# Two more tiles transposed by a DMA out of DRAM instead of on TensorE, and what is loaded around them

## The chip, the cores and the metric

The kernel runs on one core of one Trainium2 chip. The metric is the device time of one execution in microseconds (us). The profile is of one execution, taken by the hardware profiler. Engines are named as the profile names them: PE is TensorE's matmuls and PEld its weight loads, DVE is VectorE, ACT is ScalarE, POOL is GpSimd, and SP is SyncE, which here only issues DMAs.

## The reference

One block of a token-mixing MLP on x of 2048 rows by 512 columns, bf16:

```python
h = gelu(layernorm(x) @ w1)                       # 512 -> 512
g0, g1, g2, g3 = four column quarters of h, shifted along the rows by +1, -1, +2, -2 (zeros come in)
x1 = x + concat(g0, g1, g2, g3) @ w2              # 512 -> 512
out = x1 + gelu(layernorm(x1) @ w3) @ w4          # 512 -> 1792 -> 512
```

The layer norms have no weights; gelu is the tanh approximation.

## The kernel before, in words

The 2048 rows are 16 tiles of 128 (row 16p + t is partition p of tile t, line 183), so a shift along the rows by 1 or 2 is mostly a shift from tile to tile. Weights, x and all stages stay in SBUF.

A matmul contracts over partitions, so each tile of x has to be transposed (`xnT`) ahead of the matmul with w1. There are two ways to the first layer:

- *Raw tiles*, 0 to 5 (R = 6, line 180). x itself is transposed, not its norm: on PE (`tp`, line 314, four 128x128 transposes a tile, copied out of PSUM by `ev` on ACT, line 328) for tiles 0 to 3, or by a DMA out of DRAM (`tdma_x`, line 349, two tiles in one DMA, named `tdx_`) for tiles 4 and 5. `m1r` (line 374) multiplies with w1, `rc` (line 387, ACT) copies the result to SBUF as `yraw`. The norm is made up for later: `zr` (line 391, DVE) takes off mean times the column sums of w1 (`cs`, line 363, copied out by `cse`, line 369), `g1r` (line 397, ACT) scales by rstd and applies gelu, and `tdma_h` (line 355, `th_`) transposes the result into `hT`.
- *Normed tiles*, 6 to 15. Statistics (`st`, line 286, then `ag`, line 292) and the norm (`nm`, line 304) are DVE's, the inverse root (`rs`, line 297) is POOL's. `xn` is transposed by a DMA out of SBUF (`tdma`, line 338, `td0_`; pairs 6, 12, 14) or on PE (`tp8`, `tp10`, pairs 8 and 10). `m1p` (line 404) multiplies two tiles at once, `g1p` or `g1s` (lines 417, 424) apply gelu into `hT`.

The second layer (`m2s`, line 444, and `m2`, line 429) reads the shifted neighbours of a tile in `hT`: the normed tiles 8 to 15 come first, and of the raw tiles they need only 0 and 1, in the last three matmuls of that group. `x1` (line 458, DVE) adds x. Tiles of x1 are normed, transposed by DMA (`td1_`) and go through w3 (`m3h`, line 484, and `m3`, line 464) and w4 (`m4`, line 507) in blocks of four tiles; `fin` (line 519) adds x1 and stores.

The statistics of the raw tiles are needed only by `zr` and `rs`, so they are spread over DVE's time; they read x as it was loaded, so each raw tile that is transposed out of DRAM is loaded as well (`load_x`, line 271, `ldx`).

Each operation is an `Op` with the resources that it reads and writes (line 35). `firsts` (lines 633 to 648) writes out the order of the operations on each engine by hand; whatever it doesn't name follows in the order of its creation. `arrange` (line 38) merges the five lists, `emit` (line 84) turns the dependences into semaphore waits. An engine goes through its list strictly in order, SP too: a DMA whose data isn't ready holds back those listed behind it. All loads and DMA transposes go through SP, except ldw10, ldw12 and ldx1, which ACT issues. PSUM banks are fixed by hand (tp0 to tp3 in banks 6 and 7, the column sums in bank 4, which `m1p8` uses next).

Of the kernel before, what the change touches and what calls it, by code (L numbers as in the profile page):

```python
# [171 lines left out]
def bass_standalone__mixer_s_mlp__prompt_kernel(nc: bass.Bass, x, w1, w2, w3, w4, out):  # L172
# [15 lines left out]
    with ExitStack() as es:  # L188
# [82 lines left out]
        def load_x(t, n, eng="sp"):  # L271
            add(eng, f"ldx{t}", lambda e: e.dma_start(x_sb[:, t : t + n, :], xd[:, t : t + n, :]),
                writes=[(("x", i), 0) for i in range(t, t + n)], dma=True)
# [40 lines left out]
        def tp(t, n, b, raw):  # L314
            src = x_sb if raw else xn
            rd = [(("x", i), 0) if raw else (("xn", i), 0) for i in range(t, t + n)]

            def f(e):
                ins = None
                for i in range(n):  # L320
                    for c in range(DC):
                        o = 1024 * b + (i * DC + c) * P
                        ins = e.transpose(psb[:, o : o + P], src[:, t + i, P * c : P * (c + 1)], ident[:])  # L323
                return ins

            add("pe", f"tp{t}", f, reads=rd + [("ident", 1)], writes=bres(b, 1, f"tp{t}"))

        def ev(t, n, b, eng="act"):
            src = psb[:, 1024 * b : 1024 * b + n * D]
            dst = xnT[:, t : t + n, :, :].rearrange("p t c s -> p (t c s)")  # L330
            if eng == "act":
                f = lambda e: e.activation(dst, src, ACT_F.Copy)  # L332
            else:
                f = lambda e: e.tensor_copy(dst, src)
            add(eng, f"ev{t}", f, reads=bres(b, 1, f"tp{t}"), writes=[(("xT", i), 0) for i in range(t, t + n)])
# [13 lines left out]
        def tdma_x(t):  # L349
            add("sp", f"tdx_{t}",  # L350
                lambda e: e.dma_start(xnT[:, t : t + 2, :, :].rearrange("p t c s -> p (t c) s"),
                                      xd[:, t : t + 2, :].rearrange("p t d -> p (t d)"), transpose=True),
                writes=[(("xT", i), 0) for i in (t, t + 1)], dma=True)
# [20 lines left out]
        def m1r(t, b, c0=0, c1=DC):  # L374
            def f(e):
                ins = None
                for c in range(c0, c1):
                    ins = e.matmul(bank(b), xnT[:, t, c, :], w1_sb[:, c, :], start=(c == 0), stop=(c == DC - 1))  # L378
                return ins

            rd = [(("xT", t), 0)] + W1[c0:c1]
            if c0:
                rd += bres(b, 1, f"m1r{t}{c0}")
            end = f"{c1}" if c1 < DC else ""
            add("pe", f"m1r{t}{end}", f, reads=rd, writes=bres(b, 1, f"m1r{t}{end}"))

        def rc(t, b):
            add("act", f"rc{t}", lambda e: e.activation(yraw[:, t, :], bank(b), ACT_F.Copy),
                reads=bres(b, 1, f"m1r{t}"), writes=[(("yraw", t), 0)])
# [168 lines left out]
        load_w1(2, "act")  # L558
        load_w1(3, "sp")
        load_x(1, 1, "act")  # L560
        for t, n in ((6, 1), (7, 1), (2, 1), (8, 1), (3, 1), (9, 1), (10, 1), (11, 1), (12, 1), (13, 1), (14, 1), (15, 1), (4, 2)):
            load_x(t, n)
        for c in range(DC):
            load_w2(c)
# [7 lines left out]
            colsum(4, c)  # L572
        colsum_out(4)
        for t in range(R):
            if t < 4:
                tp(t, 1, 6 + t % 2, True)
                ev(t, 1, 6 + t % 2, "act")
            elif t == 4:
                tdma_x(t)
            cuts = [0, 1, 2, 3, 4] if t == 0 else [0, 2, 4] if t == 1 else [0, 4]  # L580
            for c0, c1 in zip(cuts, cuts[1:]):
                m1r(t, YB[t], c0, c1)
            rc(t, YB[t])
# [39 lines left out]
        for t in (8, 10):  # L623
# [7 lines left out]
            tdma(1, t, 2)  # L631

        firsts = {}
        firsts["pe"] = """wu tp0 cs0 cs1 m1r01 m1r02 tp1 m1r03 cs2 m1r0 cs tp2 m1r12 m1r1 tp3 m1r2 m1r3 m1r4 m1r5 tp8 m1p6
            tp10 m1p8 m1p10 m2_8a m2_9a m2_8 m2_9b m2_9 m2_10a m2_11a m2_12a m2_13a m1p12 m1p14 m2_10 m2_11
            m2_12b m2_13b m2_14a m2_15a m2_12 m2_13 m2_14b m2_15b m2_14 m2_15""".split()
        firsts["act"] = """ldw10 ldw12 ldx1 table ev0 ev1 rc0 ev2 ev3 rc1 rc2 rc3 rc4 rc5 ev8 cse g1p6 ev10 g1p8 g1s10 g1s11
            g1r0 g1r1 g1p12 g1p14 g2h_0_0_0 g2h_0_0_4 g1r2 g1r3 g2h_0_0_8 g2h_0_0_12 g1r4 g1r5""".split()
        firsts["dve"] = """pada padb padc padd pade padf st0_0 st0_6 st0_7 ag0_6 ag0_7
            st0_8 nm0_6 nm0_7 st0_9 ag0_8 ag0_9 st0_10 st0_11 nm0_8 nm0_9 ag0_10 ag0_11  # L640
            st0_12 nm0_10 nm0_11 st0_13 ag0_12 ag0_13 st0_14 st0_15 ag0_14 ag0_15 nm0_12 nm0_13 st0_1 ag0_0 ag0_1
            nm0_14 nm0_15 zr0 zr1 x1_8 x1_9 st1_8 st1_9 ag1_8 ag1_9 st0_2 nm1_8 nm1_9 st0_3 ag0_2 ag0_3 x1_10 x1_11 st1_10
            st1_11 ag1_10 ag1_11 x1_12 nm1_10 nm1_11 x1_13 x1_14 x1_15 zr2 zr3 st0_4 st0_5 ag0_4 ag0_5 zr4 zr5
            st1_12 st1_13 ag1_12 ag1_13""".split()
        firsts["pool"] = """ident0 ident1 neghalf stz ste rs0_6 rs0_8 rs0_10
            rs0_12 rs0_14 rs0_0 rs1_8 rs0_2 rs1_10""".split()
        firsts["sp"] = """ldx0 ldw11 ldx6 ldw13 ldx7 ldx2 ldx8 ldx3 ldx9 tdx_4 ldx10 ldx11 ldx12 td0_6 ldx13 ldx14 ldx15 ldw20 ldw21 ldw22 ldw23 td0_12 td0_14 ldw3a0 ldw3a1
            ldw3a2 ldw3a3 th_0 td1_8 ldw3b0 ldw3b1 ldw3b2 ldw3b3 ldx4 td1_10 th_2 th_4 td1_12 td1_14 ldw4""".split()

        slots = [4, 0, 2]  # L650
        ns = [0]
# [110 lines left out]
```

## Time and profile before

| what | value |
|---|---|
| median of 3 runs | 136.63 us (136.59 to 136.76) |
| the profiled execution | 136.71 us |
| its span, first to last instruction | 134.7 us |
| PE busy | 131.6 us, 98% of the span |
| DVE, ACT, POOL busy | 43%, 35%, 9% |
| granted TensorE clock | 1.00 in the whole span |
| read from HBM, written | 6.82 MB, 2.10 MB |

The page has six parts: busy time by engine, the span in 40 slices, the DMA queues, the chain of work that ended last, the costliest groups of instructions, and the DMA issues. In a timeline a row is the start, the length, the engine, the line of the code, the operation, what it writes and reads, and in brackets how long the engine was idle before it and what ended that. A PE matmul's length includes its passage through the pipeline, so matmuls in a row overlap in the rows; the start of one to the start of the next is what each costs. In the DMA issues the last number is the time from the issue to the landing of the last byte.

### The profile page before, as it was taken

How to read it: one execution, taken by the hardware profiler on the slowest of the kernel's cores; microseconds unless marked ns; L12 is line 12 of the kernel's file. 1: busy time of each engine (PE TensorE's matmuls, PEld its weight loads, DVE VectorE, ACT ScalarE, POOL GpSimd, SP SyncE). 2: the span in 40 equal slices, each digit the busy share in tenths (PEclk: the TensorE clock that was granted, in tenths of full speed). 3: DMA queues.
4: the chain of work that ended last, by engine and by line, in shares of the span. 5: the costliest groups of instructions: out<-in, count | busy, mean ns of one | idle time of the engine just before them, and what ended most of it. 6: DMA issues, size and time to landing. Idle time of an engine off the chain costs nothing.

```text
span 134.7 us, 1809 instructions
## 1 busy us (share of the span) xinstructions
PE 131.6 (98%) x729; PEld 69.7 (52%) x729; DVE 58.2 (43%) x135; ACT 46.7 (35%) x56; POOL 12.5 (9%) x25
## 2 busy tenths in 40 slices
PE   7999999999999999999999999999999999999993
PEld 2446867668884444444444444444444444444452
DVE  0689989799967777762222000122200002322222
ACT  3387871507963035550001555200066630000000
POOL 2032422220330012220000000000000000000000
PEclk9999999999999999999999999999999999999999
DMA  3999489984465893444111000011110001111121
GB/s 110 335 230 198 145 160 246 243 276 95 78 124 101 260 298 75 81 80 78 39 61 56 5 0 0 0 39 39 39 39 5 0 0 39 39 39 39 42 76 43
DMA packets 24568, 12.96 MB, mean 96 GB/s; under 512 B 16752, under 2 KB 23920, under 8 KB 24560
## 3 DMA queue, kind: packets, MB, share of 16 engines
q1 hardware_dynamic: 23984, 12.42, 36.4%
q10 hardware_dynamic: 576, 0.43, 1.0%
q8 instruction: 6, 0.10, 0.3%
q14 instruction: 2, 0.02, 0.1%
HBM read 6.82 MB, written 2.10 MB: 66 GB/s over the span
## 4 chain that ended last, share of the span: by engine, by line
PE 98%; DVE 0%; issue 0%
PE ps L511 36%; PE ps L468 27%; PE ps L492 9%; PE ps L410 6%; PE ps L436 5%; PE ps L450 5%; PE ps L378 4%; PE ps L534 2%; PE ps L323 2%; PE ps L366 1%; DVE o_sb L523 0%
## 5 line engine op out<-in xcount | busy, mean ns | idle before, releaser
L511 PE MATMUL ps<-w_sb,h2T 128*128 128x512 bf16 (+2 forms) x238 | 48.9, 366 | 0.0
L523 DVE TENSOR_TENSOR o_sb<-ps,x_sb 128x512 bf16<-128x512 f32 (+2 forms) x17 | 11.2, 660 | 61.2 <-PE ps L511 61.2
L479 ACT ACTIVATE h2T<-ps 128x1024 bf16<-128x1024 f32 x21 | 21.5, 1024 | 46.2 <-PE ps L468 46.2
L468 PE MATMUL ps<-x1nT,w_sb 128*128 128x512 bf16 x168 | 36.8, 379 | 0.0
L511 PEld LDWEIGHTS ps<-w_sb,h2T 128*128 128x128 bf16 x238 | 22.8, 98 | 25.9
L468 PEld LDWEIGHTS ps<-x1nT,w_sb 128*128 128x128 bf16 x168 | 16.4, 98 | 19.8
L289 DVE BATCH_NORM_STATS2 st<-x_sb 128x6 f32<-128x512 bf16 x32 | 20.9, 681 | 3.9 <-DMA x_sb<-in_x_dram 3.9
L300 POOL TENSOR_TENSOR rstd<-mv,neghalf 128x2 f32<-128x2 f32 x16 | 11.6, 725 | 46.2 <-DVE mv L294 46.2
L492 PE MATMUL ps<-x1nT,w_sb 128*128 128x256 bf16 x112 | 12.4, 273 | 0.0
L460 DVE TENSOR_TENSOR x_sb<-ps,x_sb 128x512 bf16<-128x512 f32 x16 | 10.6, 686 | 2.9 <-PE ps L436 1.5
L492 PEld LDWEIGHTS ps<-x1nT,w_sb 128*128 128x128 bf16 x112 | 10.9, 98 | 1.6
L410 PE MATMUL ps<-xnT,w_sb 128*128 128x256 bf16 x80 | 9.2, 273 | 0.0
L503 ACT ACTIVATE h2T<-ps 128x1024 bf16<-128x1024 f32 (+1 forms) x8 | 7.1, 915 | 6.0 <-PE ps L492 6.0
L410 PEld LDWEIGHTS ps<-xnT,w_sb 128*128 128x128 bf16 x80 | 7.7, 98 | 1.2
L309 DVE TENSOR_SCALAR x1n<-x_sb,mv,rstd 128x512 bf16<-128x512 bf16 x16 | 5.9, 411 | 5.3 <-POOL rstd L300 5.3
L450 PE MATMUL ps<-w_sb,hTf 128*128 128x512 bf16 x32 | 7.2, 379 | 0.0
L436 PE MATMUL ps<-w_sb,hTf 128*128 128x512 bf16 x32 | 7.1, 379 | 0.0
L378 PE MATMUL ps<-w_sb,xnT 128*128 128x512 bf16 x24 | 6.4, 399 | 0.0
L420 ACT ACTIVATE hTf<-ps 128x1024 bf16<-128x1024 f32 x4 | 4.1, 1024 | 4.1 <-PE ps L410 4.1
L332 ACT ACTIVATE xnT<-ps 128x512 bf16<-128x512 bf16 (+1 forms) x6 | 4.4, 736 | 2.6 <-PE ps L323 2.6
L294 DVE BATCH_NORM_AGGREGATE mv<-st 128x2 f32<-128x9 f32 x32 | 5.0, 186 | 0.0
L436 PEld LDWEIGHTS ps<-w_sb,hTf 128*128 128x128 bf16 x32 | 3.1, 98 | 3.6
(28 smaller groups left out, 37.1 us busy)
## 6 DMA issues: line engine op xcount, KB each, us to landing
out_dram<-o_sb SPq DMA_DIRECT2D x15, 128.0 KB, 1.8
w_sb<-in_w_dram SPq DMA_DIRECT2D x1, 1792.0 KB, 8.0
x_sb<-in_x_dram SPq DMA_DIRECT2D x13, 128.0 KB, 3.2
w_sb<-in_w_dram SPq DMA_DIRECT2D x4, 256.0 KB, 4.4
w_sb<-in_w_dram SPq DMA_DIRECT2D x6, 128.0 KB, 3.1
w_sb<-in_w_dram SPq DMA_DIRECT2D x4, 192.0 KB, 3.1
w_sb<-in_w_dram ACTq DMA_DIRECT2D x2, 128.0 KB, 3.3
x_sb<-in_x_dram SPq DMA_DIRECT2D x1, 256.0 KB, 3.9
```

Of the source, the lines that this page charges most:

```text
L289: add("dve", f"st{layer}_{t}", lambda e: e.bn_stats(st9[:, i, 0:6], src[:, t, :]), reads=[(r, 0)], writes=[(("st6", i), 0)])
L300: lambda e: e.tensor_tensor(rstd[:, i : i + n], mv[:, i : i + n, 1], neghalf[:, 0:n], ALU.pow),
L378: ins = e.matmul(bank(b), xnT[:, t, c, :], w1_sb[:, c, :], start=(c == 0), stop=(c == DC - 1))
L410: ins = e.matmul(dst, w1_sb[:, c, P * fc : P * (fc + 1)], xnT[:, t : t + 2, c, :], start=(c == 0), stop=(c == DC - 1))
L436: ins = e.matmul(bank(b), hTf[:, c0 : c0 + P], w2_sb[:, j, :], start=(j == 0), stop=(j == DC - 1))
L450: ins = e.matmul(bank(b), hTf[:, w[0] : w[0] + P], w2_sb[:, j, :], start=first and n == 0, stop=last and n == len(js) - 1)
L460: lambda e: e.tensor_tensor(x1_sb[:, t, :], bank(b), x_sb[:, t, :], ALU.add),
L468: ins = e.matmul(bank(b), w3_sb[:, c, P * fc : P * (fc + 1)], x1nT[:, 4 * q : 4 * q + 4, c, :], start=(c == 0), stop=(c == DC - 1))
L479: lambda e: e.activation(h2T[:, fc : fc + 2, q % 2, :], src, ACT_F.Gelu_apprx_tanh),
L492: ins = e.matmul(dst, w3_sb[:, c, P * (fc + i) : P * (fc + i + 1)], x1nT[:, t : t + 2, c, :], start=(c == 0), stop=(c == DC - 1))
L511: ins = e.matmul(ps[:, 512 * b : 512 * b + c1 - c0], h2T[:, fc, q % 2, P * i : P * (i + 1)], w4_sb[:, fc, c0:c1], start=(fc == 0), stop=(f ...
L523: lambda e: e.tensor_tensor(o_sb[:, k % 4, c0:c1], ps[:, 512 * b : 512 * b + c1 - c0], x1_sb[:, t, c0:c1], ALU.add),
```

## The change

Tiles 2 and 3 are transposed as tiles 4 and 5 are: one DMA, `tdx_2`, out of DRAM into `xnT`. Their transposes on PE (`tp2`, `tp3`) and the copies on ACT (`ev2`, `ev3`) go. Their plain loads (`ldx2`, `ldx3`), so far early in SP's list, and that of tiles 4 and 5 (`ldx4`, so far behind `ldw3b3`), become one load of four tiles, `ldx2`, behind `ldw23`. In SP's list ldx6, ldx7 and ldx8 stand ahead of `tdx_2`, and ldw13 behind ldx7; ldx12 goes behind `td0_6`. On DVE, `st0_1` goes from behind `nm0_13` to behind `ag0_9`, `st0_10` and `st0_11` are split by `nm0_8` and `nm0_9`, and `st0_2` takes a place ahead of `nm0_14`. On ACT, `cse` goes from behind `ev8` to behind `rc1`. PE's list loses tp2 and tp3 and is otherwise the same; POOL's is the same.

```diff
-        for t, n in ((6, 1), (7, 1), (2, 1), (8, 1), (3, 1), (9, 1), (10, 1), (11, 1), (12, 1), (13, 1), (14, 1), (15, 1), (4, 2)):
+        for t, n in ((6, 1), (7, 1), (8, 1), (9, 1), (10, 1), (11, 1), (12, 1), (13, 1), (14, 1), (15, 1), (2, 4)):
             load_x(t, n)
...
         for t in range(R):
-            if t < 4:
+            if t < 2:
                 tp(t, 1, 6 + t % 2, True)
                 ev(t, 1, 6 + t % 2, "act")
-            elif t == 4:
+            elif t % 2 == 0:
                 tdma_x(t)
...
-        firsts["pe"] = """wu tp0 cs0 cs1 m1r01 m1r02 tp1 m1r03 cs2 m1r0 cs tp2 m1r12 m1r1 tp3 m1r2 m1r3 m1r4 m1r5 tp8 m1p6
+        firsts["pe"] = """wu tp0 cs0 cs1 m1r01 m1r02 tp1 m1r03 cs2 m1r0 cs m1r12 m1r1 m1r2 m1r3 m1r4 m1r5 tp8 m1p6
...
-        firsts["act"] = """ldw10 ldw12 ldx1 table ev0 ev1 rc0 ev2 ev3 rc1 rc2 rc3 rc4 rc5 ev8 cse g1p6 ev10 g1p8 g1s10 g1s11
+        firsts["act"] = """ldw10 ldw12 ldx1 table ev0 ev1 rc0 rc1 cse rc2 rc3 rc4 rc5 ev8 g1p6 ev10 g1p8 g1s10 g1s11
...
-            st0_8 nm0_6 nm0_7 st0_9 ag0_8 ag0_9 st0_10 st0_11 nm0_8 nm0_9 ag0_10 ag0_11
-            st0_12 nm0_10 nm0_11 st0_13 ag0_12 ag0_13 st0_14 st0_15 ag0_14 ag0_15 nm0_12 nm0_13 st0_1 ag0_0 ag0_1
-            nm0_14 nm0_15 zr0 zr1 x1_8 x1_9 st1_8 st1_9 ag1_8 ag1_9 st0_2 nm1_8 nm1_9 st0_3 ag0_2 ag0_3 x1_10 x1_11 st1_10
+            st0_8 nm0_6 nm0_7 st0_9 ag0_8 ag0_9 st0_1 st0_10 nm0_8 nm0_9 st0_11 ag0_10 ag0_11
+            st0_12 nm0_10 nm0_11 st0_13 ag0_12 ag0_13 st0_14 st0_15 ag0_14 ag0_15 nm0_12 nm0_13 ag0_0 ag0_1 st0_2
+            nm0_14 nm0_15 zr0 zr1 x1_8 x1_9 st1_8 st1_9 ag1_8 ag1_9 nm1_8 nm1_9 st0_3 ag0_2 ag0_3 x1_10 x1_11 st1_10
...
-        firsts["sp"] = """ldx0 ldw11 ldx6 ldw13 ldx7 ldx2 ldx8 ldx3 ldx9 tdx_4 ldx10 ldx11 ldx12 td0_6 ldx13 ldx14 ldx15 ldw20 ldw21 ldw22 ldw23 td0_12 td0_14 ldw3a0 ldw3a1
-            ldw3a2 ldw3a3 th_0 td1_8 ldw3b0 ldw3b1 ldw3b2 ldw3b3 ldx4 td1_10 th_2 th_4 td1_12 td1_14 ldw4""".split()
+        firsts["sp"] = """ldx0 ldw11 ldx6 ldx7 ldw13 ldx8 tdx_2 ldx9 tdx_4 ldx10 ldx11 td0_6 ldx12 ldx13 ldx14 ldx15 ldw20 ldw21 ldw22 ldw23 ldx2 td0_12 td0_14 ldw3a0 ldw3a1
+            ldw3a2 ldw3a3 th_0 td1_8 ldw3b0 ldw3b1 ldw3b2 ldw3b3 td1_10 th_2 th_4 td1_12 td1_14 ldw4""".split()
```

## The prediction

> **What bounds the kernel now.** I read the page first: the shares of the engines and the chain that ended last.
>
> ```profile
> PE 131.6 (98%) x729; PEld 69.7 (52%) x729; DVE 58.2 (43%) x135; ACT 46.7 (35%) x56; POOL 12.5 (9%) x25
> ...
> PE 98%; DVE 0%; issue 0%
> ```
>
> TensorE (PE) has no gap worth naming from 0.8 us to the end, so two things alone can move the time: PE work that goes away, and a gap that the change opens in a stream that has none. The second view is PE's timeline, for the work that goes.
>
> ```profile
> 7.06 0.39 PE L323 MATMUL ps<-ident,x_sb 128*128 128x128 bf16 x4
> 7.28 1.03 PE L378 MATMUL ps<-w_sb,xnT 128*128 128x512 bf16 x4
> 8.14 0.39 PE L323 MATMUL ps<-ident,x_sb 128*128 128x128 bf16 x4
> ...
> 11.82 0.61 PE L323 MATMUL ps<-ident,xn 128*128 128x128 bf16 x8
> ```
>
> Columns: start, length, engine, line. The transposes of raw tiles 2 and 3 (tp2, tp3) start 0.22 us ahead of what follows them (7.06 to 7.28, 8.14 to 8.37): that is what each costs. The third view is VectorE's (DVE's) timeline, the fourth that of SP, which issues nearly all loads.
>
> ```profile
> 9.64 1.29 DVE L289 BATCH_NORM_STATS2 st<-x_sb 128x6 f32<-128x512 bf16 x2 [0.23 <-DMA x_sb<-in_x_dram]
> 10.85 0.72 DVE L309 TENSOR_SCALAR xn<-x_sb,mv,rstd 128x512 bf16<-128x512 bf16 x2
> ...
> 16.03 0.68 DVE L289 BATCH_NORM_STATS2 st<-x_sb 128x6 f32<-128x512 bf16 x1
> ...
> 17.47 1.41 DVE L393 SCALAR_TENSOR_TENSOR zraw<-ncs,mv,yraw 128x512 f32<-128x512 f32 x2
> 19.46 1.29 DVE L460 TENSOR_TENSOR x_sb<-ps,x_sb 128x512 bf16<-128x512 f32 x2 [0.58 <-PE ps L450]
> ```
>
> ```profile
> 5.01 1.39 SPq L351 DMA_TRANSPOSE xnT<-in_x_dram  x1
> 6.45 1.52 SPq L272 DMA_DIRECT2D x_sb<-in_x_dram  x3
> 8.60 1.26 SPq L343 DMA_TRANSPOSE xnT<-xn  x1
> 9.91 1.60 SPq L272 DMA_DIRECT2D x_sb<-in_x_dram  x3
> 11.55 1.86 SPq L546 DMA_DIRECT2D w_sb<-in_w_dram  x4
> ...
> 23.74 1.34 SPq L343 DMA_TRANSPOSE x1nT<-x1n  x1
> ```
>
> The reader is to see three things. DVE already waits for loads (tile 10's statistics at 9.64). It has little slack: from 9.64 to 19.4 us it pauses for 0.24 us (before 12.54) and for the 0.58 us before 19.46, and for nothing else over 0.15. And SP spends 1.39 us to issue a DMA transpose, against 0.47 for a plain load. The last view is the DMA issues (KB, us from issue to landing) and, of the stretch 15.4 to 17.0 us, the queues.
>
> ```profile
> xnT<-in_x_dram SPq DMA_TRANSPOSE x1, 4.2
> ...
> x_sb<-in_x_dram SPq DMA_DIRECT2D x1, 256.0 KB, 3.9
> ...
> w_sb<-in_w_dram SPq DMA_DIRECT2D x1, 1792.0 KB, 8.0
> ```
>
> ```profile
> q8 instruction: 1, 0.02, 5.2%
> ```
>
> **The parts, step by step.**
>
> 1. *PE.* tp2 and tp3 go: 2 x 0.22 = 0.44 us off the chain. Nothing is added to PE. This is the whole of what can be won, 0.3% of 136.7.
>
> 2. *ACT.* Two copies out of PSUM (ev2, ev3, 0.60 us each) go, and the 0.60 us copy cse moves ahead of rc2. ACT is idle for 65% of the span and waits for PE here; I count nothing. The first matmul of tile 1 (m1r12) loses the cover of tp2: it needs ev1, which ends at 6.99, and its slot without tp2 is 7.06. It fits, with 0.05 us to spare.
>
> 3. *SP, early.* Issues of 0.47 us each, counted on from 2.13: ldx7, ldw13 2.61, ldx8 3.08, tdx_2 3.56, ldx9 5.00, tdx_4 5.62, ldx10 7.06, ldx11 7.68. ldw13 comes 0.48 us later (it landed 3.5 us after issue, so 6.1); its first matmul is at 6.6: nothing. tdx_2 needs its landing by 7.9 (the slot of tile 2's first matmul, 8.37 less the 0.44), tdx_4 by 9.6. For a transpose out of DRAM there is one row, 4.2 us, and bounds from the nearest: 3.3 (transposes out of SBUF, L343) to 5.2 (L357, behind four weight loads). That gives 6.9 to 8.8 and 8.9 to 10.8. I take 4.2, the same operation in the same crowd: 7.8 and 9.8. So tile 2 fits and tile 4 is late by about 0.2.
>
> 4. *The queue behind them.* ldx10 is issued 0.6 later than now (7.06 for 6.45). It now lands 3.2 after issue, behind one transpose, so 10.2; by the ends of the L272 rows, 2.7 and 3.6, 9.8 to 10.7. Tile 10's statistics stand ahead of nm0_8 and nm0_9 on DVE: 0.61 (half of 9.64 to 10.85) and 0.72 later both are done, at 11.5. tp8, which now starts at 11.82, could start at 11.38, and starts at about 11.6. ldx12 has moved behind td0_6 (which goes out at 8.3 instead of 8.60: tile 7 is loaded 0.48 us earlier, of which DVE, busy with tile 6, takes up 0.3): issue 9.6, landing 2.7 to 3.2 later, 12.3 to 12.8, then 1.33 on DVE, 13.6 to 14.1. tp10 is at 14.01 now. So of the 0.44 us, what is left at tp10 is 0.4 to a loss of 0.2; I take 0.1 left. That the load takes the place of the transposes as what PE waits for is the main thing here.
>
> Weighed against the Trainium skill: from 17.30 to 18.50 us, with a transpose alone on the engines, they moved 198 GB/s, 1.3 us for its 256 KB. "DMA: Bandwidth & Descriptors", section "Latency and other measured facts", gives 261 GB/s for a DMA transpose, which would be an estimated 1.0 us; the trace does not agree, and by the page's figure tdx_4 and ldx10 would land some 0.3 to 0.6 us earlier and nearly all of the 0.44 would stay.
>
> 5. *ldx2, 512 KB.* Tiles 2 to 5 come as one load behind ldw23, and st0_2 has moved ahead of nm0_14 on DVE. DVE would reach it at about 16.8: its place there is now 16.03, and step 4 moves the work ahead of it by 0.3 to 0.8. SP issues it at 13.6 (ldx12 9.6, seven more at 0.48, one gap of 0.6 behind the transpose). No row has 512 KB. Between 256 KB in 3.9 and 1792 KB in 8.0 lies 4.6, so 18.2. Low end: 2.7 (the fastest plain load) plus 384 KB at the 309 GB/s of 2 to 5 us, 1.3, so 17.6. High end: the transpose issued at 29.61 landed after 4.8 us where its like takes 3.3; one instruction packet (q8) ran on one DMA engine meanwhile. The q8 row above shows such a packet in 15.4 to 17.0 as well (5.2% of 16 engines' 1.6 us, 1.3 us on one engine). If it meets ldx2, 1.5 more: 19.7. I take 18.5, the 512 KB estimate with a share of that delay.
>
> The Trainium skill, "Runtime: NRT & Kernel Launch", section "Instruction fetch mechanics", says that an engine's instructions come in 16 KiB blocks of 256, by a DMA queue of its own, "mostly hidden". The trace agrees with the block: about 250 PE records lie between two q8 packets. With 16 records fewer ahead of it, the first packet would come 0.5 to 0.9 us later by PE's pace there, nearer to ldx2's data; by the "hidden", ldx2 would land at 18.2 and the time would be that of the third rival.
>
> 6. *What waits for st0_2.* Behind it on DVE stand nm0_14, nm0_15 (and with them td0_14, four weight loads and th_0 on SP), zr0, zr1, then x1_8. With L the landing of x2: zr ends at L + 2.6 (0.60 from one start to the next for the statistics, 0.61 for the pair of nm, 1.41 for the pair of zr), x1_8 starts then, nm1_9 ends 4.25 later as now (19.46 to 23.71), td1_8 is issued at L + 6.9 and lands 3.3 later, L + 10.2. The first L492 matmul, which needs it, is at 28.36 now: PE waits when L is over 18.2. th_0 is issued at L + 4.6 and takes 3.3 to 5.2: L + 7.9 to L + 9.8, needed at 27.7 by the last three L450 matmuls (0.216 us each ahead of 28.36), so it decides from L = 17.9 on at the earliest. What PE loses against now is thus L - 18.2 to L - 17.9, whatever was won before, because these times don't move with PE. At 18.5: 0.3 to 0.6; I take 0.4.
>
> 7. *ldx4 at 27.19* goes (256 KB less before the transpose at 29.61). That one lands at 34.4, and its matmul, the 57th of L492 at 0.11 us each from 28.36, is at 34.5: a gain of over 0.1 needs it to land earlier too.
>
> **Sum.** The profiled execution took 136.71 us (span 134.7 and 2.0 around it). With the x2 wait: +0.4, 137.11. The median of the runs shown, 136.63, is 0.08 below the profiled one, so I say 137.0.
>
> **The rivals.**
> - *x2 wait* (forecast), chance 0.38: +0.25 to +1.2. For it: DVE's order and 512 KB behind eight loads. Against: 1.3 us of slack between td1_8's landing (27.05) and its use, which I find just used up.
> - *The early queue overshoots*: the two transposes put ldx10, ldx12 and td0_6 further behind than 0.44, PE waits at tp8 to tp10; it decides when ldx12 lands after 12.9. Slower by 0.3 to 0.6, 137.0; chance 0.10.
> - *Won and given back*: loads land as in step 4, L under 18.2; the time is within 0.25 us, 136.6; chance 0.26. What it does on PE is then only to move a wait.
> - *The gain stays* (the other side): transposes at the low end of their landing (3.3 to 4.0), ldx12 by 12.4, L under 17.9. Minus 0.3 to 0.45: 136.3; chance 0.26. For it: 0.2 us of reserve at each weight load, and PE's order is unhurt.
>
> Faster or slower by over 0.2% (0.27 us) is about what a measurement of this kernel can tell from no change. Faster 0.26, same 0.26, slower 0.48. The likeliest case alone spans 136.9 to 137.8. Range: down to 136.2 (the gain nearly whole) and up to 137.9; left out are the last part of step 5's high end and a gain of all 0.44 and the 0.1 of step 7.
>
> That the change does not do what it says is no rival: in the order of PE's instructions the eight L323 of tiles 2 and 3 are gone, and nothing else differs.
>
> **What would show it.** L323 at x24 instead of x32 PE transposes, L351 at two with landings of about 4.2 (step 3). Tile 10's statistics at about 10.2 and a PE gap ahead of L323 at 11.4 to 11.6 (step 4). DVE idle before L289 for over 1 us at 17 to 18.5, released by the x_sb load (step 5), and a PE gap between 27.5 and 28.5, ahead of L450 or L492 (step 6). A PE stream without that gap makes the forecast wrong; x2 landing before 17.5 would do it, and so would a td1_8 that lands in under 3 us.

## The result and the profile after

| | before | after |
|---|---|---|
| median | 136.76 us (136.59 to 137.00, 9 runs) | 138.08 us (137.32 to 138.86, 9 runs) |
| the profiled execution | 136.71 | 138.86 |
| its span | 134.7 | 136.9 |
| PE instructions, busy | 729, 131.6 us | 721, 132.1 us |

After to before is 1.0095, with a 95% interval of 1.0068 to 1.0122: slower by 0.9 to 1.7 us. The forecast was 137.0, within 136.2 to 137.9. The direction was right and the size was too small. The profiled execution of after is the slowest of its nine runs, 0.78 above the median; two more executions were profiled later (below).

The page of after, engine shares and the chain that ended last:

```profile
PE 132.1 (97%) x721; PEld 69.1 (50%) x721; DVE 57.8 (42%) x135; ACT 45.8 (33%) x54; POOL 12.5 (9%) x25
...
PE 76%; DVE 9%; DMA 8%; SPq 4%; issue 1%; POOL 1%
```

PE is as busy as it was, but the chain is no longer PE's alone: DVE, a DMA and SP now hold 21% of it. Followed in order of time, the chain leaves the issues of SP, goes through one DMA (6.29 us), then through DVE to the first L492 matmul on PE. DVE's timeline shows where it enters:

```profile
16.78 0.26 DVE L294 BATCH_NORM_AGGREGATE mv<-st 128x2 f32<-128x9 f32 x2
20.48 0.69 DVE L289 BATCH_NORM_STATS2 st<-x_sb 128x6 f32<-128x512 bf16 x1 [3.44 <-DMA x_sb<-in_x_dram]
...
21.73 1.41 DVE L393 SCALAR_TENSOR_TENSOR zraw<-ncs,mv,yraw 128x512 f32<-128x512 f32 x2
23.05 1.28 DVE L460 TENSOR_TENSOR x_sb<-ps,x_sb 128x512 bf16<-128x512 f32 x2
```

DVE reaches st0_2 at 17.0 (16.8 in the forecast) and stands still for 3.44 us until tile 2's load lands. Everything behind it moves: zr0 starts at 21.73 (17.47 before), x1_8 at 23.05 (19.46 before). The load itself, in the DMA issues and in SP's timeline:

```profile
x_sb<-in_x_dram SPq DMA_DIRECT2D x1, 512.0 KB, 6.3
```

```profile
14.17 0.43 SPq L272 DMA_DIRECT2D x_sb<-in_x_dram  x1
16.89 6.18 SPq L343 DMA_TRANSPOSE xnT<-xn  x2
...
25.17 1.24 SPq L357 DMA_TRANSPOSE hTf<-hraw  x1
27.32 1.23 SPq L343 DMA_TRANSPOSE x1nT<-x1n  x1
```

ldx2 goes out at 14.17 and lands 6.3 us later, at 20.46. The row at 16.89 holds both td0_12 and td0_14: SP, also in order, stands in front of td0_14 until nm0_15 has run, so the weights of layer 3 and the transposes th_0 and td1_8 go out late as well (td1_8 at 27.32; 23.74 before). PE's timeline shows the two ends of the story:

```profile
6.08 0.61 PE L323 MATMUL ps<-ident,x_sb 128*128 128x128 bf16 x4
...
7.50 4.48 PE L378 MATMUL ps<-w_sb,xnT 128*128 128x512 bf16 x20
11.82 0.61 PE L323 MATMUL ps<-ident,xn 128*128 128x128 bf16 x8
...
14.09 0.62 PE L323 MATMUL ps<-ident,xn 128*128 128x128 bf16 x8
...
25.04 1.91 PE L410 MATMUL ps<-xnT,w_sb 128*128 128x256 bf16 x16 [1.52 <-DVE st L289]
26.78 3.73 PE L450 MATMUL ps<-w_sb,hTf 128*128 128x512 bf16 x16
30.70 12.39 PE L492 MATMUL ps<-x1nT,w_sb 128*128 128x256 bf16 x112 [0.19 <-DVE mv L294]
```

tp8 starts at 11.82, as before: nothing is left there of the 0.44 us of transposes that went. In this execution it was gone ahead of tile 1. That tile's own load landed at 6.03 (5.30 before), tp1 waited for it until 6.08 (5.86 before), and tile 1's first matmul started at 7.50 where the prediction had 7.06; from there 20 matmuls run without a gap up to tp8. Further on, PE waits 1.52 us ahead of m1p14. The bracket names a DVE signal, the last to come by the profile, but td0_14 had landed at 24.90, and in all three profiled executions of after m1p14 starts 0.13 to 0.14 us behind that landing. Then the L450 matmuls and the first L492 wait further; the first L492 starts at 30.70 instead of 28.36. That is +2.34, and the span grew by 2.2.

### The profile page after: what moved, and what is told of

Same layout as the page of the kernel before. It is cut to its first block, busy times and chain, and to the rows that moved or that the text cites. A ratio compares the mean times of both kernels' runs of the same rounds, so it can differ in the third digit from the quotient of the medians.

```text
span 136.9 us, 1791 instructions
## 1 busy us (share of the span) xinstructions
PE 132.1 (97%) x721; PEld 69.1 (50%) x721; DVE 57.8 (42%) x135; ACT 45.8 (33%) x54; POOL 12.5 (9%) x25
## 4 chain that ended last, share of the span: by engine, by line
PE 76%; DVE 9%; DMA 8%; SPq 4%; issue 1%; POOL 1%
PE ps L511 35%; PE ps L468 26%; PE ps L492 9%; DMA x_sb<-in_x_dram 8%; PE ps L436 5%; DVE st L289 4%; DVE x_sb L460 2%; SPq L272 2%; SPq L546 1%; DVE xn L309 1%; POOL rstd L300 1%; DVE zraw L393 1%; DVE mv L294 1%; DVE x1n L309 1%; SPq L343 0%
## 5 line engine op out<-in xcount | busy, mean ns | idle before, releaser
L300 POOL TENSOR_TENSOR rstd<-mv,neghalf 128x2 f32<-128x2 f32 x16 | 11.5, 722 | 48.6 <-DVE mv L294 48.5
L492 PE MATMUL ps<-x1nT,w_sb 128*128 128x256 bf16 x112 | 12.4, 273 | 0.2 <-DVE mv L294 0.2
L492 PEld LDWEIGHTS ps<-x1nT,w_sb 128*128 128x128 bf16 x112 | 10.9, 98 | 1.9 <-DVE mv L294 0.7
L450 PE MATMUL ps<-w_sb,hTf 128*128 128x512 bf16 x32 | 7.5, 380 | 0.0
L399 ACT ACTIVATE hraw<-zraw,rstd 128x512 bf16<-128x512 f32 x6 | 4.0, 716 | 3.2 <-DVE zraw L393 3.2
```

Of the source, the lines that this page charges most:

```text
L300: lambda e: e.tensor_tensor(rstd[:, i : i + n], mv[:, i : i + n, 1], neghalf[:, 0:n], ALU.pow),
L450: ins = e.matmul(bank(b), hTf[:, w[0] : w[0] + P], w2_sb[:, j, :], start=first and n == 0, stop=last and n == len(js) - 1)
L492: ins = e.matmul(dst, w3_sb[:, c, P * (fc + i) : P * (fc + i + 1)], x1nT[:, t : t + 2, c, :], start=(c == 0), stop=(c == DC - 1))
```

## The experiments

The theory: DVE is held at st0_2 by ldx2's landing, and what DVE issues behind it reaches PE late. Rivals: the DMA transposes in the front make the loss; the new order on DVE and ACT makes it by itself. In the diffs "-" is after (or the kernel named), and "kernel 1" is the kernel of experiment 1.

**1. st0_2 back in its place.** The load stays as it is in after, and so does all else.

```diff
-   ... nm0_12 nm0_13 ag0_0 ag0_1 st0_2 nm0_14 nm0_15 ... ag1_8 ag1_9 nm1_8 nm1_9 ...
+   ... nm0_12 nm0_13 ag0_0 ag0_1 nm0_14 nm0_15 ... ag1_8 ag1_9 st0_2 nm1_8 nm1_9 ...
```

> The changed kernel with one operation moved back: the statistics of tile 2 (st0_2) stand again behind ag1_9, where the kernel before has them; all loads as in the change. Theory (DVE's order hands the late landing of the 512 KB load to everything behind it): DVE reaches st0_2 at about 22.5 us, when x2 has landed at 18 to 20.5; the 1.52 us gap of PE ahead of the second pair of m1p and the one ahead of L492 go; 136.3 to 136.9. Rival 1 (the 512 KB itself, by filling the DMA engines, makes td0_12 and td0_14 late): td0_14 lands after 22.9 all the same and the time stays over 137.3. Rival 2 (the two transposes out of DRAM make the front late, and the rest only follows): tp10 starts after 14.3 and the time stays over 137.3.

Measured: 136.62 us (12 runs), 0.9996 of before [0.9981, 1.0010]. The whole loss is gone with one DVE instruction of 0.65 us moved. In its profiled execution (136.30) x2 landed at 19.02, still later than DVE's 16.8, and DVE and PE did not care. DVE's timeline, then PE's:

```profile
16.82 0.73 DVE L309 TENSOR_SCALAR xn<-x_sb,mv,rstd 128x512 bf16<-128x512 bf16 x2
17.47 1.41 DVE L393 SCALAR_TENSOR_TENSOR zraw<-ncs,mv,yraw 128x512 f32<-128x512 f32 x2
19.23 1.29 DVE L460 TENSOR_TENSOR x_sb<-ps,x_sb 128x512 bf16<-128x512 f32 x2 [0.36 <-PE ps L450]
```

```profile
11.41 0.62 PE L323 MATMUL ps<-ident,xn 128*128 128x128 bf16 x8
...
21.19 3.66 PE L410 MATMUL ps<-xnT,w_sb 128*128 128x256 bf16 x32
24.68 3.62 PE L450 MATMUL ps<-w_sb,hTf 128*128 128x512 bf16 x16
28.14 12.39 PE L492 MATMUL ps<-x1nT,w_sb 128*128 128x256 bf16 x112
```

zr0 is back at 17.47, and from tp8 on no row of PE has a bracket. This also says that the transposes in the front lose nothing against before on the median.

**2. Tile 2 in a load of its own, tiles 3 to 5 right behind it;** st0_2 stays where the change put it.

```diff
-        ... (15, 1), (2, 4)):
+        ... (15, 1), (2, 1), (3, 3)):
-   ... ldw22 ldw23 ldx2 td0_12 ...
+   ... ldw22 ldw23 ldx2 ldx3 td0_12 ...
```

> The changed kernel with the 512 KB load split in two in the same place: tile 2 alone (128 KB), then tiles 3 to 5 (384 KB) right behind it; st0_2 stays ahead of nm0_14. If the size of the load is what made x2 late: x2 lands 2.5 to 3.2 us after issue, at about 17.3, DVE waits 0.3 us or less for it, 136.4 to 136.9. If a fetch of instructions that occupies one DMA engine made it late (15 of the 16 shares of ldw23 landed by 16.45 and the last at 19.18 in the changed kernel's trace): the small load is behind the same engine and lands at 18.5 to 19.8, 137.0 to 138.0.

Measured: 137.55 us (136.68 to 137.89, 12 runs), 1.0059 [1.0040, 1.0078]. Tile 2 landed at 17.04, 3.1 us after its issue, in the profiled execution, which took 136.74, next to the shortest of the 12; there DVE waits for nothing and the first L492 is at 28.39. So the landing is what the first half of the expectation said, and the time what the second half said. On the median it mends part of the loss and stays 0.9 above before; its profile doesn't show why (see 6 and 12).

**3. The new order of DVE and ACT alone.** Loads, transposes, SP's and PE's lists as before; only after's DVE list, and cse behind rc1 on ACT.

```diff
 (against before)
-   ... rc0 ev2 ev3 rc1 rc2 rc3 rc4 rc5 ev8 cse g1p6 ...
+   ... rc0 ev2 ev3 rc1 cse rc2 rc3 rc4 rc5 ev8 g1p6 ...
-   ... st0_10 st0_11 nm0_8 nm0_9 ... nm0_13 st0_1 ag0_0 ag0_1 nm0_14 ... ag1_9 st0_2 nm1_8 ...
+   ... st0_1 st0_10 nm0_8 nm0_9 st0_11 ... nm0_13 ag0_0 ag0_1 st0_2 nm0_14 ... ag1_9 nm1_8 ...
```

> The kernel before with only DVE's and ACT's order of the change (st0_1 behind ag0_9, st0_10 and st0_11 split, st0_2 ahead of nm0_14, cse behind rc1); loads and transposes as before, so x2 is there at 6.4 us. Theory (the order costs only through x2's landing): within 0.25 us of before, 136.5 to 137.0. Rival (the order by itself delays nm0_12 to nm0_15 and with them the chain to td1_8): 137.2 or more.

Measured: 136.64 us, 0.9994 [0.9983, 1.0006]. st0_2's new place costs nothing when tile 2 is loaded early. It takes both: the place and the late load.

**4. Two tiles less behind ldw23.** On kernel 1: tiles 2 and 3 loaded behind td0_14, tiles 4 and 5 behind ldw3b3 as before.

```diff
-        ... (15, 1), (2, 4)):
+        ... (15, 1), (2, 2), (4, 2)):
-   ... ldw23 ldx2 td0_12 td0_14 ldw3a0 ... ldw3b3 td1_10 ...
+   ... ldw23 td0_12 td0_14 ldx2 ldw3a0 ... ldw3b3 ldx4 td1_10 ...
```

> The changed kernel with st0_2 back behind ag1_9 and the 512 KB load taken apart: tiles 2 and 3 (256 KB) behind td0_14, tiles 4 and 5 (256 KB) behind ldw3b3 as before. td0_12 and td0_14 have no load of x ahead of them. Theory: the front of the change alone is left; if it saves what the prediction gave it (0.1, between 0.4 and a loss of 0.2): 136.2 to 136.8, and not slower than the variant that only moves st0_2 back. Rival (the front itself is what loses): over 137.2.

Measured: 136.82 us, 1.0009 [0.9995, 1.0022], just over the 136.2 to 136.8 expected and not faster than kernel 1. The 512 KB in the queue are not what keeps kernel 1 from gaining. In its profile tdx_4 landed at 10.05, and PE waited for it:

```profile
10.10 1.90 PE L378 MATMUL ps<-w_sb,xnT 128*128 128x512 bf16 x8 [0.38 <-DMA xnT<-in_x_dram]
```

**5. An attempt to move the instruction fetch** away from ldx2: empty waits on PE ahead of tp0 (two of them make one instruction; the trace has 55).

```diff
+                    if op.name == "tp0":
+                        for _ in range(112):
+                            objs[e].wait_ge(sems["pool"], 1)
```

> The changed kernel with 56 empty instructions on PE (waits on a count long reached) behind the warm-up matmuls, while PE waits for tile 0 anyway: PE's 256-instruction blocks end 56 records earlier, so that the fetch of instructions that ran at 16.0 us, among the packets of ldw23 and ldx2, runs at 12 to 13.5 us. Loads, transposes and order as in the change. If that fetch makes up most of x2's lateness: x2 lands at 17.5 to 18.8, the time falls to 136.7 to 137.4. If 512 KB behind eight loads is enough: it lands as late as before, 137.6 to 138.4.

Measured: 140.14 us, 1.0269 [1.0245, 1.0292]. It failed as an experiment. The waits run in order, one per 0.1 us from 1.0 to 6.8, and hold up the matmuls behind them:

```profile
7.15 0.58 PE L326 MATMUL ps<-ident,x_sb 128*128 128x128 bf16 x4 [3.39 <-issue]
```

PE is 3.4 us late from there on, the fetch ran at 16.7 instead of the time that was meant, and x2 landed at 18.4. It says nothing about the fetch.

**6. Tile 2 loaded early:** 128 KB alone, ahead of the weights of layer 2; tiles 3 to 5 where ldx2 was; st0_2 where the change put it.

```diff
-   ... ldx15 ldw20 ldw21 ldw22 ldw23 ldx2 td0_12 ...
+   ... ldx15 ldx2 ldw20 ldw21 ldw22 ldw23 ldx3 td0_12 ...
```

> The changed kernel with tile 2 loaded alone (128 KB) ahead of ldw20, and tiles 3 to 5 (384 KB) behind ldw23; st0_2 keeps the change's place ahead of nm0_14. Theory (only x2's landing against DVE's arrival at st0_2, about 17, matters): x2 lands at 14.5 to 16, DVE does not wait for it, PE has no gap at m1p14 or L492: 136.4 to 136.9, as the variant with st0_2 moved back (136.62). Rival (the 384 KB still hold up td0_12 and td0_14, or the later weights w2): over 137.2.

Measured: 136.66 us, 1.0003 [0.9991, 1.0014]. Tile 2 landed at 14.91, and DVE comes to st0_2 later than that:

```profile
16.65 0.26 DVE L294 BATCH_NORM_AGGREGATE mv<-st 128x2 f32<-128x9 f32 x2
16.82 0.65 DVE L289 BATCH_NORM_STATS2 st<-x_sb 128x6 f32<-128x512 bf16 x1
```

The row has no bracket: no wait. With all 512 KB still loaded, with st0_2 still ahead of nm0_14, the loss is gone. What matters is whether tile 2 has landed when DVE comes. Kernel 2 differs from this one only in the place of tile 2's load, so its 0.9 us hangs on that place too.

**7. What the transpose costs in the front.** On kernel 1, tdx_2 is left out, and the first matmuls of tiles 2 and 3 read tiles 0 and 1, so that PE's work is the same.

```diff
-   e.matmul(bank(b), xnT[:, t, c, :], ...
+   e.matmul(bank(b), xnT[:, t if t not in (2, 3) else t - 2, c, :], ...
-   ... ldx8 tdx_2 ldx9 tdx_4 ...
+   ... ldx8 ldx9 tdx_4 ...
```

> The variant with st0_2 back behind ag1_9, and without the DMA that transposes tiles 2 and 3: their matmuls read the transposed tiles 0 and 1 instead, so what is left out is the transpose of tiles 2 and 3 on any engine. It takes the price of the DMA transpose in the front away and keeps what PE saves. If that DMA (SP's 1.39 us and 1.3 us of all DMA engines) is what takes back the 0.44: tile 10 lands at about 9.3 and the time is 136.1 to 136.35. If something else holds PE (the landing of tile 1, the norm chain of tiles 8 to 11): 136.5 to 136.7, as with it.

Measured: 136.09 us, 0.9961 [0.9947, 0.9975]: 0.5 us under before by the ratio (0.3 to 0.7), and 0.53 under kernel 1 on the medians (of two chips, whose medians of before are 0.03 apart). So removing tp2 and tp3 is worth about what step 1 said, and the DMA that does their work takes it back. In the profile ldx10, issued earlier without tdx_2 ahead of it, landed at 8.71 (10.01 in after); the front, on PE:

```profile
11.26 0.62 PE L323 MATMUL ps<-ident,xn 128*128 128x128 bf16 x8
...
13.85 0.62 PE L323 MATMUL ps<-ident,xn 128*128 128x128 bf16 x8 [0.22 <-DVE xn L309]
```

Through which wait the DMA takes it back is not shown: tp10, at 13.85, is no earlier here than in kernel 1's profile (13.79), and the two profiled executions, 136.22 and 136.30, lie closer together than the medians.

**8. nm0_8, nm0_9 ahead of st0_10 on DVE** (on kernel 1), so that tp8 doesn't wait for tile 10's load.

```diff
-   ... st0_1 st0_10 nm0_8 nm0_9 st0_11 ag0_10 ...
+   ... st0_1 nm0_8 nm0_9 st0_10 st0_11 ag0_10 ...
```

> The variant with st0_2 back behind ag1_9, and on DVE nm0_8 and nm0_9 ahead of st0_10, which waits for ldx10. If x10's landing is what PE's tp8 waits for: tp8 starts at 11.4 or earlier and the time falls by 0.1 to 0.3 against 136.62, 136.3 to 136.5. If tdx_4's landing or the later chain to tp10 (x11, x12) binds as well: no change, 136.5 to 136.7, or 0.2 more, since st0_10 and what follows come later.

Measured: 136.70 us, 1.0001 [0.9990, 1.0011]. No gain: tp8 started at 11.51, but PE had waited 0.25 for tdx_2 ahead of it and waited 0.21 at tp10 for the next xn, at 14.08. The wait only moved on.

**9. ldx12 ahead of td0_6 again** (on kernel 1).

```diff
-   ... ldx11 td0_6 ldx12 ldx13 ...
+   ... ldx11 ldx12 td0_6 ldx13 ...
```

> The variant with st0_2 back behind ag1_9, and ldx12 ahead of td0_6 in SP's list, as in the kernel before (SP is idle there for 0.5 us, since td0_6 waits for nm0_7). If tile 12's landing is what holds tp10 (13.8 in that variant, 13.57 wanted): tp10 starts 0.2 earlier, 136.3 to 136.5, and the version beats both. If td0_6 then lands 0.4 later and m1p6 waits for it instead: 136.6 to 136.9.

Measured: 136.49 us, beside 136.59 of before on the same chip; 1.0003 [0.9987, 1.0019]. No difference that can be told. In its profile PE waits 0.23 for td0_6 instead (m1p6 at 12.48), and tp10 is at 14.23, not earlier.

**10 to 12. After twice more, and kernel 2 once more,** one profiled execution each, for the spread of L, the landing of x2.

> The changed kernel once more, for a second profile: its times lie 1.5 us apart, and the theory says that x2's landing L is what differs. The execution's span should be 134.5 + (L - 18.2) for L over 18.2: 134.7 at 18.4, 135.5 at 19.2, 136.8 at 20.5. Rival (something else makes the spread, such as the front): the span does not follow L within 0.3 us.

> The changed kernel a third time, for the same test as the second profile: span 134.5 + (L - 18.2) within 0.3 us.

> The variant with tile 2 loaded alone in the same place, once more. Its first profile fell on one of its two fastest executions (x2 landed at 17.0, no loss), its median is 0.9 above before. Theory: this execution's span follows L as in the changed kernel, so a span of 135.4 or more comes with L of 18.7 to 19.5. Rival: L is 17 to 17.5 again, and td0_12, behind the 384 KB, lands after 21.3 and holds m1p12.

| execution of after | L | first L492 | against 28.36 | by step 6 | us |
|---|---|---|---|---|---|
| first | 20.46 | 30.70 | +2.34 | +2.26 to +2.56 | 138.86 |
| second | 20.64 | 32.02 | +3.66 | +2.44 to +2.74 | 140.18 |
| third | 18.94 | 30.15 | +1.79 | +0.74 to +1.04 | 138.31 |

The test that was set, a span within 0.3 us of 134.5 + (L - 18.2), fails in both repeats of after: 138.2 us where it gives 136.9, and 136.4 where it gives 135.2. So L alone does not make the spread. On PE, the formula of step 6 holds for the first execution and is about 0.8 to 0.9 short, by its upper end, in the others. PE's timeline of the third:

```profile
23.57 1.91 PE L410 MATMUL ps<-xnT,w_sb 128*128 128x256 bf16 x16 [0.57 <-DMA xnT<-xn]
...
29.14 0.82 PE L450 MATMUL ps<-w_sb,hTf 128*128 128x512 bf16 x3 [0.85 <-DMA hTf<-hraw]
30.15 12.06 PE L492 MATMUL ps<-x1nT,w_sb 128*128 128x256 bf16 x109 [0.19 <-DMA x1nT<-x1n]
```

th_0 holds the last three L450, and td1_8 comes only just behind it. Both went out within 0.1 us of what the formula says (th_0 at L + 4.7, td1_8 at L + 6.9, in all three). What differs is the time to land: 5.4 and 5.6 us for th_0 in the third and second, 4.5 in the first; 4.2 and 4.4 for td1_8, 3.2 in the first, and SP spent 2.2 and 2.4 us on td1_8's issue instead of 1.2.

Kernel 2's second profiled execution took 137.12: tile 2 landed at 16.72 and DVE did not wait, but the front was slow (tp8 at 12.05, waiting 0.17 for xn). That is neither what the theory expected of L and of the time nor the late td0_12 of the rival (m1p12 did not wait for it). Neither profile of kernel 2 shows a run near its median of 137.55, so what that median is made of stays open.

## Why the prediction was wrong in size

1. *PE, 0.44.* Right: with nothing in its place the removal is worth 0.5 (kernel 7 against before, 0.3 to 0.7).

2. *ACT.* Right: kernel 3 shows no cost of the moved cse. PE did not wait for ev1 in after.

3. *tdx_2 at 7.8, tdx_4 at 9.8.* They landed at 8.28 (4.7 after issue) and 9.62 (4.1). The bounds held; tile 2 was the late one. ldw13, put at 6.1 and at no cost, landed at 6.4 to 6.5 in after's three profiles and held PE by 0.1 us in the third.

4. *0.1 left of 0.44.* The number held: tp10 is at 14.09, 13.87 and 13.69 in after's three profiles (14.01 before), and kernel 1 against before, 136.62 to 136.68, says the same on the median. So did most of the reason. By the ends of DVE's rows, the norms that tp8 and tp10 need were ready at 11.54 and 14.03 in the first profile (forecast 11.5, and 13.6 to 14.1); in the kernel before they were ready at 11.57 and 13.28, 0.25 and 0.73 ahead of PE. At tp10 it was the load, as named: DVE waited 0.33 us for tile 12's. At tp8 it was not: tile 10 had landed at 10.01, and DVE was still at st0_1, which the change had put ahead of it. Two waits were not foreseen. In the first execution the whole 0.44 was gone at tile 1, whose load landed at 6.03; in kernel 3, with the loads of before, it landed at 6.10, so this lateness doesn't need the change. In the third, tdx_2 landed at 7.99 and held PE by 0.29. Kernel 7 shows that leaving tdx_2 out is worth 0.5 on the median (ldx10 then lands 1.3 us earlier), but not through which wait. By the 261 GB/s of the Trainium skill's "DMA: Bandwidth & Descriptors" (section "Latency and other measured facts") nearly all of the 0.44 would have stayed, as the prediction estimated. The runs do not agree: kernel 1 has 0.06 of it.

5. *ldx2 lands at 18.5.* This step failed. The issue was forecast at 13.6 and was at 13.6 to 14.2 in after's three profiles; the time to land was taken as 4.9 (4.6 by interpolation, with a share of the delay by a fetch) and was 6.3, 6.6 and 5.3. The high end, 19.7, was passed in two of three. The same 512 KB load took 4.4, 4.6, 5.0, 5.5 and 6.0 us in kernels 8, 5, 1, 7 and 9. So 4.6 was about the best case, not the middle. The load is divided over 16 DMA engines and counts as landed with the last: in the first profile 15 shares were there by 18.79 and the last at 20.46; in the second 14 by 18.56 and two at 20.51 and 20.64. The instruction packet on q8 ran at 16.0 to 18.0 and at 17.4 to 18.35 in these two, and at 14.9 to 16.0 in the third, where the last share was only 0.7 behind the others. The first fits a fetch that delays the share of the engine it runs on. As a rule the traces don't bear it out: in the second, two shares were late and one packet ran, and in kernels 5 and 8 a packet at 16.7 to 17.6 and at 16.9 to 17.8, in the middle of the same load, left the last share 0.4 behind, with the two earliest landings of the eight. The attempt to move the packet failed (kernel 5), so what makes a share late stays open. The rule quoted from the Trainium skill ("Runtime: NRT & Kernel Launch", section "Instruction fetch mechanics"), "mostly hidden", speaks of the cost of crossing into the next block; no run here shows whether a load beside the fetch pays for it.

6. *L - 18.2 to L - 17.9.* The mechanism is shown by kernels 1, 3 and 6 together: the loss is gone when st0_2 stands behind ag1_9, and also when it stands ahead of nm0_14 and tile 2 lands early; after has the place and the late load. The price was too low, and this is the second term that failed. The step took td1_8 at 3.3 us to land and th_0 at up to 5.2, where two of three profiles had 4.2 to 4.4 and 5.4 to 5.6. With these, the loss is L - 17.2 to L - 17.0 (18.94 - 1.79, 20.64 - 3.66). Such times are no exception: over the fourteen profiles of all kernels td1_8 took 3.1 to 4.5 us, 3.7 in the median, so the one row of before was nearer the best case than the middle here as well. The list of PE's waits also left out td0_14, which follows from the same L and cost 1.52 us at m1p14 in the first profile; that wait was no extra loss, since the same chain ends later, at L492.

7. *ldx4 gone.* No gain is visible, 0.06 us at most: the loss at L492 is passed on to the end (from the first L492 to the end 106.22 us, 106.29 before).

The sum of the prediction, 136.71 + 0.4, becomes 136.71 + 2.26 = 138.97 for the profiled execution (138.86 measured) when the measured L of 20.46 stands in step 6's formula in place of 18.5: 20.46 - 18.2 = 2.26. The median, 138.08, is 1.3 above before, and no profile fell on it: it fits an L of about 18.4 by the price of the second and third profile, or 19.4 by the first's (20.46 - 2.34 = 18.12). An estimate from medians: the 512 KB load landed at 19.2 over its eight profiles (after's three and kernels 1, 5, 7, 8 and 9), and with td1_8 at 3.7 us step 6 gives 19.2 + 6.9 + 3.7 - 28.36 = 1.4. By this estimate both terms made the miss, L with some 0.7 (19.2 for 18.5) and td1_8 with some 0.4 (3.7 for 3.3).

The rivals: *early queue overshoots* fell (kernel 1 has both transposes in the front and is level with before). *Won and given back* is what kernels 1 and 6 do, and what after would be without the wait. *The gain stays* fell too: it needed the transposes at the low end of their landing.

No version here beats before by more than the measurement tells; kernel 7 does, but it leaves work out.

## What to carry to other kernels

An instruction put into an in-order engine's list hands the lateness of its own input to all that stands behind it, however small it is: ask of each moved statistic or copy when its load lands in a bad execution, not in the interpolated one, and keep it behind the work that others wait for until then. A load divided over many DMA engines is as late as its slowest share, so a large load needs more reserve than its size says; if one tile of it is wanted early, load that tile alone and earlier. Work moved from a full engine to a DMA in a crowded stretch can be paid for in full there: here 0.44 us saved on PE was taken back on the median, through waits that differ from one execution to the next.

## What the runs showed of the hardware beyond that

- Three profiled executions of one program took 138.3 to 140.2 us, with the clock granted at 1.00 in all; the difference is in when shares of one load and two transposes landed. The loss grows to 3.7 us at L492 by that alone.
- Instructions on PE that wait for a semaphore already reached are not free: 55 of them took one slot of 0.1 us each, 5.8 us, of which 3.4 were not covered by the matmuls ahead (kernel 5).
- SP's issue of one DMA transpose of the same shape took 1.23 us or 2.2 to 2.4 us, and where it took longer it also landed a microsecond later. What held it back stays open.
